# State read then routed attention on one core: z leaves its bank in one multiplication, mask and zeros share a tile, and a new order table

## The chip, the cores and the metric

The kernel runs on one core of a Trainium2 chip. Five queues work side by side: PE (matmuls), DVE and ACT (elementwise work; both read the matmul banks), POOL (elementwise work between on-chip tiles) and SP, which issues the DMAs. The metric is device microseconds (us) of one execution. Before the change the median of three runs is 297.14 us (296.94 to 297.83). The profile is of one further execution that took 296.96 us.

## The reference

```python
# x: 8 batches x 8 heads x 512 tokens x 64; state: 8 x 8 x 32 x 64
a     = softmax(scale * x @ state.T);  xread = a @ state      # tokens read the state
a2    = softmax(scale * state @ x.T);  sread = a2 @ x         # the state reads the tokens
x     = concat([xread, sread])         # 8 batches, 544 tokens, 512 wide
logits = x @ w_gate                    # 4 experts; each token takes its best 2
w      = softmax over the two chosen logits
for e in range(4):                     # causal attention of width 64 per expert
    ye   = softmax(causal(scale * (x @ wq[e]) @ (x @ wk[e]).T)) @ (x @ wv[e]) @ wo[e]
    out += (w of expert e, 0 where it is not chosen) * ye
```

A token has two chosen experts, its two "slots". The kernel sorts them so that slot 0 holds expert 1, 2 or 3 and slot 1 holds expert 0, 1 or 2, and computes two softmax rows for a token instead of four.

## The kernel before

A batch goes through four kinds of work. The *front* computes the state softmax `eb` (row maximum `mb`, exponential, row sum `sbm`, product with its reciprocal), turns it into `at`, and forms the products `gs` of state and weights, the values `v`, the keys `kt`, the queries `qf`/`qh`/`qm`, the gate and its weights `wgt`. The *side* work computes the other softmax (`mr`, `m`, `e`, `a`, `a2t`) and the 32 state tokens. The *main* work goes through the four 128-token blocks i of the batch: `probs` computes the masked scores of both slots (`p`, `mx`), the exponentials, a high and a low half (`ph`) and a DMA that transposes them (`pt`). `reads` multiplies `pt` by `v` into one bank: 193 columns per slot, 192 for three experts and one column of row sums. From there `su` (row sums), its reciprocal and `c6` (named `c` in rows; weight over row sum, three columns per slot) follow, then `z`, its halves `zh`, a DMA transpose, the product with `wo_n`, and the store of `o`. A *tail* handles the state tokens of two batches. In the last batch three blocks turn z on PE (`ident,z`) and skip the DMA.

Every number is a high and a low 16-bit half, so most products are three matmuls. There are 32 `reads`, eight batches of four blocks.

In `reads` before the change, z is made in four instructions out of one bank. Lines 907 to 910 multiply slot 1 by its three weights (one DVE instruction, or three on ACT). Lines 911 and 912 multiply the third expert of slot 0 (ACT or DVE). Lines 913 to 915 multiply the other two of slot 0 and add them onto slot 1 (two DVE instructions). In rows, z is the tile `z6` until its halves are taken.

The order is not found at run time. The functions only record steps (class `Steps`); a step may have several ways, say DVE or ACT, and `run` emits all steps in the sequence of a stored table `ORDER`. That table holds the sequence of steps, the way of each, and the buffer slot of each tile. So every queue follows a fixed list, and an engine waits at the head of its list. `FILL` is a list of start times for single matmuls over a tile of zeros, which have no result anyone reads; the table puts them mostly near the start. All instructions are emitted from line 268.

Of the kernel before, what the change touches and what calls it, by code (L numbers as in the profile page):

```python
# [18 lines left out]
CFG = dict(FILL=(1.0, 1.4, 1.8, 2.2, 2.6, 3.0, 3.4, 3.8, 4.2, 4.6, 5.0, 5.4, 5.8, 6.2, 6.6, 7.0, 7.4, 7.8, 8.2, 8.6, 9.0, 9.4, 9.8, 10.2, 10.6, 11.0, 11.4, 11.8, 12.2, 12.6, 13.0, 13.4, 13.8, 14.2, 14.6, 15.0, 15.4, 15.8, 16.2, 16.6, 17.0,), RA=-1, RG=1, RV=2, RK=2, ZL=3, GP=1, PT=4, ZM=4, SM=4, QM=4, SIDE=32, FB=1, PX=1, PA=2, LB=1, xn=4, W0=-33, PACE=37.0, LAG=2,  # L19
# [1096 lines left out]
```

## Time and profile before

| | before |
|---|---|
| median of 3 runs | 297.14 us |
| profiled execution | 296.96 us |
| its span, first to last instruction | 295.2 us |
| PE busy | 279.0 us, 95% of the span |
| DVE busy | 251.6 us, 85% |
| ACT busy | 218.0 us, 74% |
| POOL busy | 173.3 us, 59% |
| granted TensorE clock | 1.00 in every slice |

The profiled execution has 1.76 us outside its span. Busy time says how long an engine was at work, whether or not anyone waited for it; the idle time before an instruction and its releaser say who was late.

### The profile page before, as it was taken

The numbers are of one execution on the slowest core, as the hardware profiler recorded it, in microseconds if no ns is written. First come the engines' busy times: TensorE is split into PE (matmuls) and PEld (weight loads), VectorE is DVE, ScalarE is ACT, GpSimd is POOL, SyncE is SP. The second block draws the span as 40 slices with busy tenths as digits, with TensorE's granted clock in tenths as the row PEclk, the third lists the DMA queues.
The fourth block names the chain that finished last, engine by engine and source line by source line (L and its number), as shares of the span: only waits on it lengthen the run. The fifth ranks groups of instructions, "written<-read, shape, count | busy, mean of one in ns | idle before, by whom it ended". The sixth has DMA issues, their size and how long they took to land. (4 is left out here: it accounts for less than half of the span.)

```text
span 295.2 us, 9038 instructions
## 1 busy us (share of the span) xinstructions
PE 279.0 (95%) x3318; PEld 185.3 (63%) x3318; DVE 251.6 (85%) x821; ACT 218.0 (74%) x611; POOL 173.3 (59%) x245
## 2 busy tenths in 40 slices
PE   7899899998899899999999999999999999999895
PEld 3755555665576557576665777665777667844753
DVE  2788999999799889998889999898899996798552
ACT  3877687996699798898869986998684636646442
POOL 5773644678793786797657988496627535213000
PEclk9999999999999999999999999999999999999999
DMA  6997999999899999999999999998998877649954
GB/s 184 247 194 128 192 196 193 203 195 205 156 214 205 163 173 205 219 194 246 168 212 203 195 203 163 179 218 160 159 236 144 118 189 100 109 115 176 180 201 178
DMA packets 165564, 54.01 MB, mean 183 GB/s; under 512 B 144400, under 2 KB 161040, under 8 KB 165520
## 3 DMA queue, kind: packets, MB, share of 16 engines
q1 hardware_dynamic: 165520, 53.44, 93.9%
q8 instruction: 26, 0.43, 0.6%
q14 instruction: 18, 0.15, 0.1%
HBM read 11.08 MB, written 8.91 MB: 68 GB/s over the span
## 5 line engine op out<-in xcount | busy, mean ns | idle before, releaser
L268 PE MATMUL bank<-gs,at 128*128 128x260 f16 (+3 forms) x368 | 50.9, 283 | 0.5 <-DVE mx L268 0.4
L268 PE MATMUL bank<-kt,qm 128*128 128x128 f16 (+7 forms) x384 | 45.5, 299 | 1.1 <-DVE gs L268 1.1
L268 PE MATMUL bank<-v,pt 128*128 128x193 f16 x480 | 44.5, 246 | 1.9 <-DMA pt<-ph 1.8
L268 PE MATMUL bank<-wo_n,z 128*128 128x512 f16 (+1 forms) x198 | 45.4, 373 | 0.0
L268 PEld LDWEIGHTS <-pt 128*128 128x128 f16 x480 | 40.0, 97 | 5.1 <-DMA pt<-ph 2.5
L268 POOL TENSOR_TENSOR ph<-p,ph 128x768 f16<-128x768 f32 (+1 forms) x18 | 33.0, 1834 | 13.1 <-DVE gs L268 4.3
L268 ACT ACTIVATE p<-p,mx 128x256 f32<-128x256 f32 (+3 forms) x64 | 33.6, 555 | 7.7 <-DVE mx L268 4.5
L268 PEld LDWEIGHTS <-at 128*128 128x128 f16 x336 | 31.7, 97 | 9.2 <-issue 2.1
L268 PEld LDWEIGHTS <-qm 128*128 128x128 f16 (+1 forms) x384 | 22.8, 96 | 20.6 <-issue 9.3
L268 PEld LDWEIGHTS <-z 128*128 128x128 f16 x198 | 18.5, 97 | 19.5 <-issue 1.6
L268 DVE CUSTOM_DVE_ANT_0 p<-bank,maskb 128x128 f32<-128x128 f32 (+3 forms) x64 | 28.8, 480 | 0.2
L268 ACT ACTIVATE z<-bank,c 128x64 f32<-128x64 f32 x75 | 19.5, 319 | 11.5 <-POOL c L268 4.6
L268 PE MATMUL bank<-at,gs 128*128 128x512 f16 (+1 forms) x92 | 24.3, 399 | 1.2 <-DVE eb L268 0.9
L268 POOL TENSOR_TENSOR qh<-qf,qh 128x768 f16<-128x768 f32 x12 | 19.9, 1661 | 6.3 <-ACT qh L268 3.5
L268 ACT ACTIVATE o<-bank 128x512 f32<-128x512 f32 (+1 forms) x29 | 16.7, 586 | 5.3 <-PE bank L268 5.2
L268 POOL TENSOR_TENSOR eb<-eb,sbm 128x512 f32<-128x512 f32 x14 | 15.3, 1099 | 7.9 <-PE bank L268 3.9
L268 DVE SCALAR_TENSOR_TENSOR z<-bank,c,z 128x64 f32<-128x64 f32 x64 | 16.5, 274 | 3.9 <-ACT z L268 2.8
L268 ACT ACTIVATE xh<-xn 128x512 f16<-128x512 f32 x32 | 19.4, 630 | 0.0
L268 POOL TENSOR_TENSOR zh<-z,zh 128x256 f16<-128x256 f32 x20 | 14.3, 714 | 8.6 <-ACT zh L268 4.4
L268 POOL TENSOR_TENSOR c<-su,wgt 128x6 f32<-128x6 f32 x24 | 6.1, 255 | 20.7 <-DVE su L268 16.2
L268 DVE SCALAR_TENSOR_TENSOR xh<-xn,xh 128x512 f16<-128x512 f32 x23 | 16.5, 719 | 0.2 <-ACT xh L268 0.2
L268 ACT ACTIVATE ph<-p 128x768 f16<-128x768 f32 (+1 forms) x15 | 13.9, 927 | 3.1 <-DMA pt<-ph 3.0
(222 smaller groups left out, 643.7 us busy)
## 6 DMA issues: line engine op xcount, KB each, us to landing
out_dram<-o SPq DMA_DIRECT2D x33, 256.0 KB, 2.7
xn<-in_x_dram SPq DMA_DIRECT2D x16, 512.0 KB, 4.8
sn<-in_state_dram SPq DMA_DIRECT2D x9, 64.0 KB, 3.8
p<-in_moe_wo_dram SPq DMA_DIRECT2D x4, 128.0 KB, 2.8
z<-zh SPq DMA_TRANSPOSE x29, 3.2
xT<-xh SPq DMA_TRANSPOSE x28, 3.3
p<-in_moe_wv_dram SPq DMA_DIRECT2D x1, 384.0 KB, 5.3
p<-in_moe_wk_dram SPq DMA_DIRECT2D x1, 384.0 KB, 6.3
```

What stands on the lines that cost most here:

```text
L268: f(**{k: v.ap() if isinstance(v, View) else v for k, v in kw.items()})
```

## The change

Four edits. (1) In `reads` both slots are multiplied by their weights in one instruction (DVE: 384 columns out of the bank; or ACT: six of 64 columns), and the two experts that both slots may hold are added inside the on-chip tile, 128 columns, on POOL or DVE. The expert order inside z turns by one place, so `wo` is loaded in its own order (two DMAs of 128 rows instead of four of 64) and the tail picks its columns one place further. (2) The mask tile becomes the last 128 columns of the zeros tile. (3) `FILL` has 34 entries instead of 41. (4) The order table is a new one for the whole program: sequence, ways and slots. The `maskb` step, `probs` and `tail` change in column numbers only.

```diff
--- before.py
+++ after.py
@@ -16,62 +16,60 @@
 ALU = mybir.AluOpType
 AX = mybir.AxisListType

-CFG = dict(FILL=(1.0, 1.4, 1.8,
...
-15.8, 16.2, 16.6, 17.0,), RA=-1, RG=1,
...
+CFG = dict(FILL=(1.0, 1.4, 1.8,
...
+13.0, 13.4, 13.8, 14.2,), RA=-1, RG=1,
...
            FRONT=1.5, FSPAN=1.0, TSPAN=1.3, TOFF=1.2, KT=3, p32=3, ph=2, at=1, et=1, gs=1, xh=4, a2=1, o=4, sn=1, qf=2,
            n_eb=1, n_e2=1, n_a2t=1, n_xt_tail=2, n_z32=3, n_z=2, n_zh=3, n_tq=1, n_tv=2, n_tpt=2, n_tz=2)
 ORDER = (
     (
-        "c-jruV`C5s6adico0p9(+jgsE+qP}HwrtzBZQHhOzxN}~htnL2
...
+        "c-jq@gO(5q6acSpwbf>8+ict0X4|%Hd$VoZwr$(Cjraax&Y77i
...
     ),
     (
...
     ),
 )
 MASK = -1e30
@@ -301,8 +299,10 @@
     st = Steps(nc, sb, psum)


-    zeros = const.tile([P, DM], BF16, name="zeros")
+    band = const.tile([P, DM + P], BF16, name="band")
+    zeros = band[:, :DM]
     nc.vector.memset(zeros, 0.0)
+    st.tags["maskb"] = [band]
     ident = const.tile([P, P], F32, name="ident")
     make_identity(nc, ident)
     identh = const.tile([P, P], F16, name="identh")
@@ -396,9 +396,9 @@

     def constants():

-        maskb = st.buf("maskb", [P, S], BF16)
-        fill(maskb, 0.0)
-        select(maskb[:, S - P:], ALU.is_ge, MASK, 0, [[-1, P]], 1)
+        maskb = st.buf("maskb", [P, DM + P], BF16)
+        fill(maskb[:, DM:], 0.0)
+        select(maskb[:, DM:], ALU.is_ge, MASK, 0, [[-1, P]], 1)

         rows = [(c, s, slice((2 * c + s) * NS, (2 * c + s + 1) * NS)) for c in range(NB) for s in range(2)]
         mtail = st.buf("mtail", [P, P], BF16)
@@ -484,8 +484,7 @@
     def load_wo(after):
         for pr in range(E // 2):
             wof = stage()
-            for h in range(2):
-                st.dma(wof[h * D:(h + 1) * D, :DM], wo[(2 * pr + 1 + h) % E], 0.4, after=after)
+            st.dma(wof[:, :DM], wo[2 * pr:2 * pr + 2].rearrange("e d m -> (e d) m"), 0.8, after=after)
             hi_lo(DM, wo_n[:, 0, pr, :], wo_n[:, 1, pr, :], wof[:, :DM], 256.0, psum=False)

     tz, e2s = {}, {}
@@ -871,7 +870,7 @@
         for k, i in enumerate(unit):
             for s in range(2):
                 o = 2 * at_[i] + s * w_[i]
-                masked(w_[i], p32[:, o:o + w_[i]], part[s, i], consts["maskb"][:, S - w_[i]:], mx[:, 2 * k + s:2 * k + s + 1])
+                masked(w_[i], p32[:, o:o + w_[i]], part[s, i], consts["maskb"][:, DM + P - w_[i]:], mx[:, 2 * k + s:2 * k + s + 1])
         shifted(2 * nb, mx)
         for k, i in enumerate(unit):
             for s in range(2):
@@ -887,7 +886,7 @@
     def reads(b, i):
         v, w6 = vs[b], c6s.pop((b, i))
         pt, k0 = pts.pop((b, i))
-        z32 = st.buf("z6", [P, E * D], F32, bufs=CFG["n_z32"])
+        z6 = st.buf("z6", [P, 2, 3 * D], F32, bufs=CFG["n_z32"])

         zp = bank("zp")
         W = 3 * D
@@ -895,24 +894,21 @@
         for s in range(2):
             g += chain((zp[:, s * (W + 1):(s + 1) * (W + 1)], pt[:, c, k0 + s * (i + 1) + j, :], v[:, a, j, V0 - s + (1 - s) * D:V0 + 1 - s + (1 - s) * D + W])
                        for j in range(i + 1) for a, c in PROD)
-        st.mm(g, (len(g), W + 1, 128, 1), into=[z32])
+        st.mm(g, (len(g), W + 1, 128, 1), into=[z6])
         su = st.buf("su", [P, 2], F32, bufs=4)
         c6 = st.buf("c6", [P, 2, 3], F32, bufs=4)
         tiny(2, su, zp[:, W:W + 2], EPS * 2.0 ** 15)
         dve(28, nc.vector.reciprocal, out=su, in_=su)
         pair(6, out=c6, in0=su.unsqueeze(2).broadcast_to([P, 2, 3]), in1=w6.rearrange("p (s e) -> p s e", s=2), op=ALU.mult)

-        r = [zp[:, :W], zp[:, W + 2:2 * W + 2]]
-        o = z32[:, :W]
-        st.either([("DVE", 0.264, (nc.vector.tensor_tensor, dict(out=o.rearrange("p (e d) -> p e d", e=3), in0=r[1].rearrange("p (e d) -> p e d", e=3),
-                                                                in1=c6[:, 1, :].unsqueeze(2).broadcast_to([P, 3, D]), op=ALU.mult))),
-                   ("ACT", 0.595, *((nc.scalar.activation, dict(out=z32[:, e * D:(e + 1) * D], in_=r[1][:, e * D:(e + 1) * D],
-                                                               func=AF.Copy, scale=c6[:, 1, e:e + 1])) for e in range(3)))])
-        st.either([("ACT", 0.2, (nc.scalar.activation, dict(out=z32[:, W:], in_=r[0][:, 2 * D:], func=AF.Copy, scale=c6[:, 0, 2:3]))),
-                   ("DVE", 0.2, (nc.vector.tensor_scalar, dict(out=z32[:, W:], in0=r[0][:, 2 * D:], scalar1=c6[:, 0, 2:3], scalar2=None, op0=ALU.mult)))])
-        for e in range(2):
-            o = z32[:, (e + 1) * D:(e + 2) * D]
-            dve(D, nc.vector.scalar_tensor_tensor, out=o, in0=r[0][:, e * D:(e + 1) * D], scalar=c6[:, 0, e:e + 1], in1=o, op0=ALU.mult, op1=ALU.add)
+        by = "p s (e d) -> p s e d"
+        st.either([("DVE", 0.465, (nc.vector.tensor_tensor, dict(out=z6.rearrange(by, e=3), in0=zp.windows((W + 2, 2), (D, 3), (1, D)),
+                                                                in1=c6.unsqueeze(3).broadcast_to([P, 2, 3, D]), op=ALU.mult))),
+                   ("ACT", 1.19, *((nc.scalar.activation, dict(out=z6[:, s, e * D:(e + 1) * D], in_=zp[:, s * (W + 2) + e * D:s * (W + 2) + (e + 1) * D],
+                                                              func=AF.Copy, scale=c6[:, s, e:e + 1])) for s in range(2) for e in range(3)))])
+        kw = dict(out=z6[:, 1, D:], in0=z6[:, 1, D:], in1=z6[:, 0, :2 * D], op=ALU.add)
+        st.either([("POOL", 0.39, (nc.gpsimd.tensor_tensor, kw)), ("DVE", 0.2, (nc.vector.tensor_tensor, kw))])
+        z32 = z6.rearrange("p s c -> p (s c)")[:, 2 * D:]
         z = st.buf("z", [P, 2, 2, P], F16, bufs=CFG["n_z"])
         if b == B - 1 and i < CFG["ZL"]:

@@ -1047,7 +1043,7 @@
         zt = bank("zt")
         g = []
         for e in range(E):
-            o = e * D
+            o = (e + E - 1) % E * D
             g.append((zt[e % 2 * D:(e % 2 + 1) * D, e // 2 * N:(e // 2 + 1) * N].rearrange("p (n c) -> p n c", c=NB), zr[:, o:o + D],
                       consts["both"].rearrange("p (c n) -> p n c", c=NB), True, True))
         st.mm(g, (4, 4 * N, 128, 2), into=part)
```

What the new table does to the instruction counts (rows of each queue counted by kind, before and after): DVE has 50 instructions fewer, ACT 7, POOL 3, SP 2, PE the 7 zeros matmuls with their weight loads; PE's other matmuls are the same. The 32 z blocks were made by 64 scalar-tensor-tensor, 15 tensor-tensor of 192 columns and 8 tensor-scalar instructions on DVE and 75 on ACT; now by 22 tensor-tensor of 384 columns on DVE, 60 on ACT (ten blocks), and 32 additions, 18 on DVE and 14 on POOL.

The DVE queue at the start, in the first batch's front, before the change (`eb` is the state softmax, `sbm` its row sums, `mr` and `m` the row maxima of the other softmax, `gs` the gate and value products):

```order
L268 TENSOR_REDUCE sbm_120<-eb_116 128x16
L268 TENSOR_REDUCE mr_150<-bank_80 128x2
L268 TENSOR_REDUCE mr_150<-bank_81 128x2
L268 TENSOR_SCALAR sbm_120<-sbm_120 128x16
L268 RECIPROCAL sbm_120<-sbm_120 128x16
L268 TENSOR_TENSOR m_1_147<-mr_150 128x2
L268 TENSOR_REDUCE sbm_120<-eb_116 128x16
L268 SCALAR_TENSOR_TENSOR xh_96<-xn_87,xh_96 128x512
L268 TENSOR_SCALAR gs_122<-bank_83 128x260
L268 SCALAR_TENSOR_TENSOR wn_75<-p_1_114,wn_75 128x4x64
L268 TENSOR_SCALAR gs_122<-bank_77 128x260
L268 RECIPROCAL sbm_120<-sbm_120 128x16
```

The same place after the change:

```order
L266 TENSOR_REDUCE mr_149<-bank_83 128x2
L266 TENSOR_REDUCE mr_149<-bank_78 128x2
L266 TENSOR_TENSOR m_1_146<-mr_149 128x2
L266 TENSOR_REDUCE sbm_118<-eb_115 128x16 x2
L266 RECIPROCAL sbm_118<-sbm_118 128x16
L266 TENSOR_SCALAR sbm_118<-sbm_118 128x16
L266 TENSOR_SCALAR gs_121<-bank_80 128x260
L266 TENSOR_SCALAR gs_121<-bank_84 128x260
L266 RECIPROCAL sbm_118<-sbm_118 128x16
L266 TENSOR_TENSOR eb_115<-eb_115,sbm_118 128x512
```

The two maxima reductions moved ahead of both row sums, the second `xh` and a `wn` step moved behind, and the second product of `eb` with its reciprocal, on POOL before, is now on DVE. On PE both pairs of `eb` turns stand next to each other; before, six zeros matmuls and two products stood between them.

The DVE queue in the last batch, where the last blocks leave their banks, before the change (`z_0` to `z_2` are the z6 buffers, `tz` and `tzr` belong to the tail):

```order
L268 RECIPROCAL su_171<-su_171 128x2
L268 RECIPROCAL tsu_200<-tsu_200 128x1
L268 TENSOR_TENSOR tzr_205<-bank_82,tc_1_207 128x256
L268 RECIPROCAL su_169<-su_169 128x2
L268 SCALAR_TENSOR_TENSOR z_0_165<-bank_78,c_1_173,z_0_165 128x64
L268 TENSOR_SCALAR z_2_167<-bank_84,c_2_174 128x64
L268 SCALAR_TENSOR_TENSOR z_177<-bank_77,z_177 128x256
L268 SCALAR_TENSOR_TENSOR z_0_165<-bank_78,c_1_173,z_0_165 128x64
L268 SCALAR_TENSOR_TENSOR z_2_167<-bank_84,c_2_174,z_2_167 128x64 x2
```

And after it:

```order
L266 RECIPROCAL su_169<-su_169 128x2
L266 TENSOR_TENSOR c_1_172<-su_169,wgt_125 128x6
L266 SCALAR_TENSOR_TENSOR tz_208<-bank_81,tz_208 128x64x2
L266 TENSOR_TENSOR z_2_166<-bank_82,c_1_172 128x384
L266 TENSOR_SCALAR su_170<-bank_78 128x2
L266 TENSOR_TENSOR z_2_166<-z_2_166 128x128
L266 TENSOR_TENSOR z_1_165<-bank_77,c_3_174 128x384
L266 RECIPROCAL su_170<-su_170 128x2
L266 TENSOR_TENSOR c_3_174<-su_170,wgt_125 128x6
L266 TENSOR_TENSOR z_2_166<-bank_78,c_3_174 128x384
L266 TENSOR_TENSOR z_2_166<-z_2_166 128x128
```

DVE now makes z of a block alone, in two rows, where ACT and DVE took turns at one bank before.

## Rows read from the trace of the kernel before

**Rows 1.** Windows: head, middle, end; busy us (count) of each engine, PE clock, DMA.

```profile
core 0: us, PE busy (x) PEld busy (x) DVE busy (x) ACT busy (x) POOL busy (x), PEclk, DMA share, GB/s
0.00:45.00 45.00, 41.07 (x522) 24.65 (x522) 35.09 (x90) 31.69 (x74) 25.97 (x64) 1.00 0.96 191
45.00:240.00 195.00, 187.70 (x2339) 126.82 (x2338) 179.74 (x597) 159.01 (x449) 135.87 (x163) 1.00 1.01 188
240.00:295.20 55.20, 50.27 (x464) 33.84 (x458) 36.81 (x136) 27.28 (x89) 11.43 (x20) 1.00 0.71 160
```

**Rows 2.** Waits of PE in 45 to 240 us: total, times, longest.

```profile
PE bank L268 <- DVE gs L268: 1.3, 2, 1.1
PE bank L268 <- DMA a2t<-a: 1.2, 1, 1.2
...
PE bank L268 <- ACT z L268: 0.6, 1, 0.6
```

**Rows 3.** Groups by form: count, busy us, mean ns, idle before and releasers.

```profile
L268 ACT ACTIVATE z<-bank,c 128x64 f32<-128x64 f32 x75 | 19.5, 319 | 11.5 <-POOL c L268 4.6 <-DVE z L268 4.0 <-DVE c L268 2.9
L268 DVE SCALAR_TENSOR_TENSOR z<-bank,c,z 128x64 f32<-128x64 f32 x64 | 16.5, 274 | 3.9 <-ACT z L268 2.8 <-issue 0.7
...
L268 POOL TENSOR_TENSOR zh<-z,zh 128x256 f16<-128x256 f32 x20 | 14.3, 714 | 8.6 <-ACT zh L268 4.4 <-issue 3.5
L268 DVE TENSOR_TENSOR qf<-bank,m 128x384 f32<-128x384 f32 x26 | 13.6, 545 | 0.3
...
L268 POOL TENSOR_TENSOR c<-su,wgt 128x6 f32<-128x6 f32 x24 | 6.1, 255 | 20.7 <-DVE su L268 16.2 <-DVE tsu L268 4.0 <-DVE gt L268 0.4
L268 DVE TENSOR_TENSOR z<-bank,c 128x192 f32<-128x192 f32 x15 | 5.2, 348 | 1.1 <-ACT z L268 0.7 <-POOL c L268 0.4
...
L268 DVE TENSOR_SCALAR z<-bank,c 128x64 f32<-128x64 f32 x8 | 2.2, 279 | 0.2
...
L268 DVE TENSOR_TENSOR c<-su,wgt 128x6 f32<-128x6 f32 x8 | 1.8, 225 | 0.2
...
L268 DVE TENSOR_TENSOR eb<-eb,sbm 128x512 f32<-128x512 f32 x2 | 1.4, 684 | 0.0
```

**Rows 4.** PE in order of time, head: start us, us, idle before and releaser.

```profile
15.02 2.97 PE L268 MATMUL bank<-zeros 128*128 128x512 bf16 x13
18.40 0.66 PE L268 MATMUL bank<-ident,eb 128*128 128x128 f32 x4 [0.41 <-POOL eb L268]
...
21.27 0.66 PE L268 MATMUL bank<-ident,eb 128*128 128x128 f32 x4
```

**Rows 5.** POOL in order of time, head.

```profile
20.16 1.05 POOL L268 TENSOR_TENSOR eb<-eb,sbm 128x512 f32<-128x512 f32 x1 [0.34 <-DVE sbm L268]
```

**Rows 6.** DVE in order of time, head.

```profile
17.04 0.10 DVE L268 TENSOR_TENSOR m<-mr 128x2 f32<-128x2 f32 x1
...
17.65 1.25 DVE L268 SCALAR_TENSOR_TENSOR xh<-xn,xh 128x512 f16<-128x512 f32 x1
...
20.74 0.49 DVE L268 TENSOR_TENSOR s<-er 128x2 f32<-128x2 f32 x1 [0.66 <-ACT e L268]
```

**Rows 7.** The chain that ended last, one block of the last batch.

```profile
276.21 0.18 DVE c L268
...
276.49 0.32 ACT z L268
...
276.91 0.37 DVE z L268
...
277.81 0.29 DVE zh L268
```

**Rows 8.** Waits of PE in the last batch, in order of time.

```profile
273.60 3.68 PE L268 MATMUL bank<-v,pt 128*128 128x193 f16 x42 [1.04 <-DMA pt<-ph]
...
281.01 0.58 PE L268 MATMUL bank<-ident,z 128*128 128x128 f32 x2 [0.34 <-DVE z L268]
```

**Rows 9.** The halves of z on DVE: ns min, median, max; first and last start.

```profile
L268 DVE TENSOR_TENSOR zh<-z,zh x9: 396/417/426, 125.2 to 278.1; 128x256 f16<-128x256 f32 x9
```

More of the change, by code (lines that the diff above doesn't have):

```diff
@@ L69 @@
[L69 to L74 removed]
+        "c-jq@gO(5q6acSpwbf>8+ict0X4|%Hd$VoZwr$(Cjraax&Y77ikPPxdQb-B;AQ(zQey9)0p%8>(L)Z-f2m}lQ3I+}tAq(t<RFD<+K_<ussi8"
@@ new lines @@
+        "5Xhs=-`!a;b5009sYvO^=-18E=^<bZV00&+u6D2nAV543~|*b17!UFZx~p*3`YI#3tdKqV{z_n-_^g$!^Xib7W?2c_U3Jb<=P3<^LBs09z99"
+        "Xy3d5E%j?3PgoIPz}1lV`vYLpgVMczR(Q%!4oKh(I7g+fS3>qVnZB=3-KU6bcCAF1A0Pb>;;{mIF!WU@C*t<b0~{Vp*MuWC3p_?U^EngvhV^"
+        "9K^1%nwV^sxf>KxvC%{Rl4A<Zl6vsGp9!lUTNB{{T5hRBGa2Q_0Bp3r@;V7JeBQOHSK}8${17IMWgNYCZAut#g!v#17Q(*>7gCQ^zPQxr157"
+        "XfUEP?ef8|J`Sm<#)19$bW_P!89^P?!%3U?D7m)vyM(KxupfTVWe)fMxI&*1;{<4kIBhZG;2x4vxbpsD_(x2W*0>cpJ9iPS^~?U^8yV9XJ`P"
+        "<8qh+v1kj{z^!-(8saXfiLG%3G{T+O0ItAF2+zB)7QTnw*ckWVDo6rB@CBM+3fhacu|1}wBy=4vLkDb%!4yOtu?{9A!XHo<Q_**5gJ0nre1M"
@@ new lines @@
+        "<u8=7G<`UUkcDgA{26s(Voe;_$E$3(Ob|3L#(bnJwQX+O5W8vmo#8M|Q@Y>5Z3Eq2B3*aKT(KWvBP!7w65;KBF_`r`l$hlug0Cw_+bG!(;Q0"
+        "*Ztqus7a-D?9`T;zvkLy)X>NV`LnIV{rlw!*SRLC*nvvh?8(K4#)H~1qb0&oQ9bx5U1l>oPm9DCPw8&xC|HLIy{1DC>k%p$h;g^V+LA^5ikm"
+        "7qFI=hVsjjh&WCUf#=sT064Ox<T#xxF9~GdCG!NtQ2AqviaSq1BRTv8cc`k0m*mx8RQXGuIB`6C`p!t{%qhU$PN)ssv591_CileX;Ex^$j9f"
+        "Pqn+=PXA46{*Oj7^g%8OFox6q7IGDU8B7C_SFQoK%R8V`(~xh3PcL$Fo?5&fyfggSqGm7NPTa216)0=B8L&7>d$W%tK`<175&;c$G6^Bf5)u"
+        "=^9p`a+C`zQVPt37x6lVQe&D*O{hHGzyQ9)32++CrQBGIB61#VO3mpK=EdTa86)w1yovcR9zVoploG2^7L3og@B!ANAWq7)XgVd}L|mV0Py@"
@@ new lines @@
+        "<}y(t4H<n&yVQeiOX$2ydlE5bZVh)K9E-NuZZjH^?3u1$UDDfZy`l!+5zCF)Bjr6)I}8I%o^b1$w;nYjQy!xUT)t56HN$*J)<R;3r%n`cr5c"
+        "!@13CC{cu+?HBVJL*TR=?=fbTYN(9^J~n)?dc;v!Z+B4I#5Tt%bn;Groqls2tQ*N>Pla*8$ICcn3cQJZ5~8}sSm%!{xp=nVqgA?sdylz=EOL"
+        "Rde9K+$D^qi^`vh&oEFeyUPvS99xtL1G=RoXVO&ge=sW(yZ2XXyP!7z_VFYxIM^S$+f@ydxEhVI7M3kE!;{_SOPxuKgr?kwJkH=9SzAQqs=$"
+        "gF4m6VS2^I5shgLnm9<}0$3-eU;n;2XS(a`Je}%SwZJHLaniyoYk}TG~qmcpx|7b@Yta(+_^mFZd-l<bqt7chf8W$=BsAH|1aany*R`-bE3p"
+        "ob03W@`fwOZ!W|e=p7%RMqHl%a9XS=#rZu4&>?EZQ*}Ru@Im^^MnCWaN2Fuam=9A4jzpE@oJ6K0^pTI#Pdq_4<f3e((tMIOQ79MXe_WD_@p&"
@@ new lines @@
+        "r46}T*a;%a=9HdA%3$d&mspQ0)pNaeV)RN|_9Nu0j$X{sVM_zczjUre?5BApkM+T4=2P&lf?Tj`WspeWRuPfK0CM3<?m)Z_YGihto1YR+e5i"
+        "Z<Y{+=4ssZ;VQ9xD%hHZ`_e1NGr~Xow+TmM5FI~Q@U_FCP^&e<d&G+mf8|tx-v_9zAH)PDpeB^mpAeO?@1(iD*@7tlSo9#CHLhTy_5GcUmr?"
+        "!c_23^w?vk_5-fKlk4(~=R8wxz9IYio_#EA)N0LwOP%?QeGxdY~!5WfZa_U{mrMWe>T&E{AjE8c38NrM69tFu08P50VDaDb562^fNSLW(yo~"
+        "09b3_qZeoJU9TSbjzyD4s-@=QPX~Xaadbd3795;*YY8qDmr}r`u^Fzod^elb_0D{v@Ah2R)PLGM+zEG<hLWB)NQ{hm=AV>ujCPf9NZ{q8Rdx"
+        "X7M9>P5CsXe5W^*M(W5*iB4%Hm86sWx<q42YMIKhq=>|z^zxT}PzEU^|0ttm65u(US*Gb+&LSlxt1Q%PQb6W0azQCBpJfUcmbdgp3g~prAt9"
@@ new lines @@
+        "CuVb9?sy|kC{oL<(8cm)sfa$epmdL{o4m9M(;"
+    ),
+    (
+        "c-p;{(XPWV2tzsi|3_bSYHq*~mZwFUnxv@4U_7&5F5g?8AJ2nymlk@$ay$~2&qPc<cr5@c%GVV!7AuJF&TY=P(%wOwjuFL90GQNH^NeNAjI<"
+        "DN1^loew83<Lxj3I`Y5f<F`T=jY-Xa~S(cRS6_}Jh6J|e2}m@21C2p@RbNH0gYsQTi9@G5$_>LG<xLkrUIrV;f?7iV2Y*8NnI`^UujqNT`ed"
+        "84m1%7|bKm-P<b1m{sA3$p04>mQd+6tkX&57ef5*|6kDu{Qx>JFZnHcQt*6zlcG&MCwjU5GfFE>}G<RHQ$ZDPxattf72%c8~"
+    ),
+    (
+        "c-l>qi*7?P2t#@2|NnT$aHlPms)QPB4DJ4R;_tX;4#zmIue5l3`FA`B6D@oBfIaI9!cMrnlsP;i!N$1WDlwKFo9}{F@Oa^nrXM7e5E|N_#Ml"
+        "Hiz}hrv4e>L5+OB9j6#k^LU3Z<C5_4|JdepNH;i&<axqfz-GRqg^A~gb0Cy%dcn{<CI%!LMJ<zv?&+DUOaHOnPfdX{bLt2%U-r6dB!OY!nnG"
+        "rVF=F|n@tU!w`go9e9#BkhI#>hMaTE74>9zA33To>Cj=nLhL*OEnvQra__ora|#g1=*5zbv^to8fVw=Q85ki8==omWd}@_W)&wInf}x%W;cb"
+        "`-t8FaxvlLU`N5fD$cc9$=GyC&Z9ARX3XAhzyCt|*A$O9}NxNGt);yYInvnW&t$bA*IC>2}cjE@$zC=qP=jXdA^(_e_q%^6tL}TJXj|MxdT8"
+        "twL0qC|$?OOz(xc9ui72q#seeL)C6<kYS=XPn3>jY1rXj_kw^XOHk?)u{TEy?YA3nNZunLmCC23`"
```

64 lines of the change are left out of this document (16 added, 48 removed).

## The prediction

> **What bounds the kernel now.** I read the windows by stage first, then PE's waits, then the groups by form, and last the two ends in order of time. The windows [rows 1] show the reader three stages. In the middle, 45 to 240 us, PE is busy 187.70 of 195.00 us and DVE 179.74 (92%); PE stands still for 7.3 us and DVE for 15.3. So PE sets the time there, with DVE close behind. In the head PE is busy 41.07 of 45 us, but part of that is zeros matmuls, which fill time in which it would wait: 13 of them stand in one row of 2.97 us, 0.228 us each, and it waits 0.41 us more behind them [rows 4]. The head is a chain of latencies. In the last batch PE waits at two places of which one is z [rows 8]. PE's waits in the middle have many releasers; the two that bear on this change are DVE with 1.3 us over gs and ACT with 0.6 over z [rows 2].
>
> **z, on the three engines.** Before, DVE spends 64 x 0.274 + 15 x 0.348 + 8 x 0.279 = 17.5 + 5.2 + 2.2 = 25.0 us on z [rows 3]. After, 22 blocks cost one multiplication of 384 columns out of a bank. The query step has the same form, 0.545 us, so 12.0 us. The addition (128 columns, both inputs on chip) isn't in the trace. On DVE it lies between the tensor-tensor of 6 columns, 0.225 us, and that of 256, 0.415 [rows 3]; on the straight line between them 0.32, which I take: 18 x 0.32 = 5.8 (4.1 to 7.5). DVE falls by 25.0 - 17.8 = 7.2 us (5.5 to 8.9). ACT falls by 15 of its 75 pieces of 0.319 us, 4.8 us. POOL gains 14 additions between 0.255 us (6 columns) and 0.714 (256 columns) [rows 3]; on the line 0.48, so 6.7 us (3.6 to 10.0). POOL is busy 135.87 of 195 us in the middle [rows 1] and has that room. The other steps that change engine I cost at nothing in sum, since what leaves one engine lands on another with room.
>
> The readers of the bank also stop taking turns. In one block of the last batch [rows 7] c ends at 276.39 us, ACT makes one piece from 276.49, DVE one from 276.91, DVE two more, and z is ready at 277.81: 1.42 us. Made by DVE alone it takes 0.545 + 0.32 = 0.87 us, 0.55 less. On ACT six pieces of 0.319 plus an addition are 2.2 to 2.6 us, so ten of the 32 blocks get longer. In the groups, DVE's z pieces waited 2.8 us for ACT and ACT's 4.0 for DVE [rows 3].
>
> **Middle: -2.1 us.** Some 28 of the 32 blocks lie in it, so DVE's load falls by 28/32 x 7.2 = 6.3 us and its free time rises from 15.3 to 21.6. My estimate lets PE's waits shrink as that free time grows: 7.3 x (1 - 15.3/21.6) = 2.1. The ends are -7.3 (no visible wait is left) and +5 (below, the port).
>
> **Head: -1.2 us.** The list of DVE shows the second product of the state softmax coming sooner. Before, DVE ran an xh step of 1.25 us between the second row sum and its reciprocal [rows 6], and POOL needed 1.05 us for the product [rows 5], so PE turned the second half at 21.27, 2.87 us after the first [rows 4]. The new list has xh behind and the product on DVE, 0.684 us [rows 3]: 1.25 + (1.05 - 0.68) = 1.6 us sooner. The seven zeros matmuls that go are 7 x 0.228 = 1.6 us as well, what PE would otherwise wait. They stood in front of late inputs and return nothing by themselves. I take 1.2, since the first half and the weights that PE needs beside it move less (0 to -2.0). What is late next is the copy of the turned half out of its bank. With the zeros gone PE may stand still a little more often; the granted clock is 1.00 in all three stages, waits included [rows 1], so I price that at nothing.
>
> **End: -0.5 us.** PE waited 0.34 us for z before a turn [rows 8], and the block chain is 0.55 shorter on DVE; the 1.04 us for the pt transfer I leave. Between +1.0 (the tail's own product is late in the new list, a z now stands before it) and -1.4 (both waits go).
>
> **Mask, zeros, wo: 0.** The mask step reads the same number of columns from another place. POOL's fill of it, 128 columns instead of 512, lies in the head, where POOL is busy 25.97 of 45 us [rows 1]. Two wo DMAs instead of four take two issues off SP; the data are needed only by the first product of z. If that cover were gone, later arrival would cost some tenths.
>
> **Sum.** Against the profiled execution of 296.96 us (span 295.2 and 1.76 around it; 0.18 below the median of 297.14): 296.96 - 1.2 - 2.1 - 0.5 = 293.2 us.
>
> **A rule against it.** A DVE instruction over two elements took 0.49 us at 20.74 and ended when POOL's product (20.16 to 21.21) did; one of the same size at 17.04 took 0.10 [rows 5, 6]. So a DVE instruction with two on-chip inputs can stand behind POOL. Before, z's additions had one input in the bank; now all 32 have both on chip. Against that, nine subtractions with two on-chip inputs on DVE took 396 to 426 ns, none stretched [rows 9]. The Trainium skill (SBUF — State Buffer, section Who interferes with whom) says that a DVE instruction with two SBUF inputs contends with a GpSimd one that reads SBUF, the loser blocking for the whole instruction. The two rows at 20 us agree with it and the nine do not show it. By that rule the additions would cost what the first rival says; by the nine rows, the sum above.
>
> **Rivals.** The port, slower: Each of DVE's 18 additions waits as that one did, 0.39 us (7.0 in all, which eats the 7.2 saved), and POOL's 14 hold DVE up for their own 6.7 us. Then DVE's free time in the middle falls to 15.3 - 28/32 x 6.7 = 9.4 us, PE's waits grow to 7.3 x 15.3/9.4 = 11.9, and the time is 296.96 - 1.2 - 0.5 + 4.6 = 299.9. It decides once the additions lose more than 7.2 us, 0.22 us each. For it: the 0.49 us. Against: the nine rows.
>
> The table does not do what it says: its waits may be no nearer to the real ones, and one fixed list of a queue then waits at its head where the old did not: PE, after one stall as long as its longest in the middle, 1.3 [rows 2], in each of three batches, and no gain there: 296.96 - 1.2 - 0.5 + 3.9 - 1.3 = 297.9. For it: the whole program was put in order again, and 8 us on DVE mean little if 1 us is lost now and then. Against: the work per engine falls.
>
> No change: PE is busy 96% of the middle; the same matmuls run, and what DVE saves turns into idle time of DVE. Zeros matmuls go where PE then waits. Only the end is left: 296.5. For it: PE's longest waits in the middle are for gs and for a transfer, not for z [rows 2].
>
> More: half the 7.3 us of waits go, and the head gives 2.0: 296.96 - 2.0 - 3.7 - 1.4 = 289.9, or less if short waits inside the rows shrink too.
>
> **How the numbers follow.** Chances: forecast 0.56 (290.5 to 296), more 0.10, no change 0.15, table 0.09, port 0.10. About 0.3% (0.9 us) is what can be told from no change. Faster takes the forecast and more, 0.66; same 0.15; slower 0.19. The range of 288.5 to 298.8 leaves out the far half of the port and the best of more.
>
> **What would show it.** Right: the second pair of eb turns within 1 us of the first; no ACT and DVE pieces of z out of one bank; z additions of 0.25 to 0.35 us on DVE; DVE's busy time in the middle down by 5 us or more; PE's waits there near 5 us. Wrong: additions of 0.6 us and more beside POOL's work, or new waits of PE above 1 us in the middle; and if DVE's busy time falls while PE's stays and its waits too, the third rival holds.

## The result and the profile after

The changed kernel takes 292.58 us in the median of 4 runs (291.49 to 294.35) against 297.1 for the kernel before on the same chip; the ratio is 0.9836, 95% interval 0.9803 to 0.987. The forecast was 293.2. The profiled execution, whose rows follow, is the longest of the four, 294.35 us with a span of 292.6; most of what it has more stands in one place, shown below.

The windows of the changed kernel, with the columns of [rows 1]:

```profile
0.00:45.00 45.00, 40.50 (x498) 25.15 (x502) 32.95 (x89) 34.05 (x84) 25.43 (x61) 1.00 0.97 190
45.00:240.00 195.00, 189.68 (x2363) 128.52 (x2362) 178.29 (x566) 165.41 (x453) 131.93 (x164) 0.99 1.02 190
240.00:292.60 52.60, 47.82 (x451) 31.72 (x449) 34.59 (x118) 23.91 (x69) 10.98 (x18) 1.00 0.72 160
```

PE stands still for 5.3 us in the middle instead of 7.3. But DVE's busy time there fell only from 179.74 to 178.29 us, and the granted clock is 0.99, not 1.00. Yet a window of fixed length holds more of a faster kernel's work (2363 matmuls here, 2339 before), so the load is better compared over the whole program: DVE is busy 245.8 us instead of 251.6, ACT 223.4 instead of 218.0, POOL 168.3 instead of 173.3. The new table gave ACT other steps, so it carries more although its part of z shrank.

The groups by form that belong to z, with the columns of [rows 3]:

```profile
L266 ACT ACTIVATE z<-bank,c 128x64 f32<-128x64 f32 x60 | 13.3, 324 | 2.5 <-POOL c L266 1.9 <-DVE c L266 0.6
L266 DVE TENSOR_TENSOR z<-bank,c 128x384 f32<-128x384 f32 x22 | 12.1, 551 | 0.5
...
L266 POOL TENSOR_TENSOR z<-z 128x128 f32<-128x128 f32 x14 | 6.8, 488 | 4.2 <-ACT z L266 2.3 <-DVE su L266 1.7
...
L266 DVE TENSOR_TENSOR z<-z 128x128 f32<-128x128 f32 x18 | 5.5, 305 | 0.1
```

All four terms are near their estimates: 551 ns (545 taken), 305 (320), 488 (480), and 60 ACT pieces. DVE spends 12.1 + 5.5 = 17.6 us on z where [rows 3] add up to 25.0. The idle time ahead of them changed more: before, DVE and ACT waited 2.8 and 4.0 us for each other at z, and now for nothing of the kind.

The waits of DVE and ACT in the middle, longest first: total, times, longest. Before:

```profile
DVE eb L268 <- ACT e L268: 2.0, 4, 0.8
DVE tv L268 <- ACT tv L268: 1.3, 1, 1.3
...
DVE p L268 <- PE bank L268: 0.4, 1, 0.4
...
ACT p L268 <- DVE mx L268: 2.7, 2, 1.9
ACT p L268 <- POOL mx L268: 2.6, 3, 1.5
```

After:

```profile
DVE p L266 <- PE bank L266: 6.7, 6, 3.9
DVE kt L266 <- ACT kt L266: 0.8, 3, 0.3
...
ACT o L266 <- PE bank L266: 3.7, 4, 1.3
ACT xh L266 <- PE bank L266: 3.2, 1, 3.2
ACT xt_tail L266 <- PE bank L266: 2.4, 2, 1.6
```

The releaser has turned. Before, the engines that empty the banks waited mostly for each other; now they wait more for PE's next bank. Summed over the middle, DVE and ACT wait 22.3 us for each other and 9.4 for PE's banks before, 12.1 and 22.5 after. The two longest waits after, 3.9 and 3.2 us, belong to the one late transfer shown next and are not the order's; in the kernel `swap` (below), whose profile has no late transfer there, the sums are 13.4 and 17.0. PE's waits for DVE and ACT fall from 4.0 us to 2.5, in `swap` to 1.8.

In the head, PE in order of time, as in [rows 4]:

```profile
18.89 1.19 PE L266 MATMUL bank<-ident,eb 128*128 128x128 f32 x8
...
33.36 0.75 PE L266 MATMUL bank<-bd,xT 64*128 64x32 f16 x47 [1.28 <-ACT v L266]
...
40.81 1.42 PE L266 MATMUL bank<-kt,qm 128*128 128x128 f16 x16
```

Both halves of eb turn in one row; the second begins near 19.5, some 1.8 us sooner than in [rows 4]. Part of it goes again at 33.36 to ACT's v, a wait that the old list did not have.

The one new long wait lies at 96.6 us; PE and SP in order of time:

```profile
93.49 1.28 SPq L266 DMA_TRANSPOSE a2t<-a  x1
...
96.36 0.27 PE L266 MATMUL bank<-ident,sn 128*128 128x128 f32 x1
...
98.78 2.54 PE L266 MATMUL bank<-a2t,xh 128*128 128x64 f16 x48 [2.15 <-DMA a2t<-a]
...
101.25 1.41 PE L266 MATMUL bank<-wn,bd 64*32 64x512 f16 x24
```

and in the windows around it:

```profile
95.00:99.00 4.00, 1.85 (x18) 0.91 (x16) 3.89 (x13) 3.13 (x10) 2.81 (x3) 1.00 1.29 122
99.00:103.00 4.00, 4.00 (x75) 2.73 (x73) 1.64 (x4) 1.57 (x4) 1.35 (x2) 0.57 1.18 248
```

PE waits 2.15 us for a transfer and starts 5.3 us after its issue, and then the granted clock falls to its lower level (1.2 of 2.4 GHz; 0.57 in the mean of 99 to 103 us): 48 matmuls a2t,xh take 2.54 us here and 1.57 in the kernel before. The runs of the changed kernel are of two kinds: 291.49 and 291.61 us at a mean clock of 1.000 and 0.998, 293.55 and 294.35 at 0.994.

### The profile page after: what moved, and what is told of

Its sections match the earlier page's. It is cut to its first block, busy times and chain, and to the rows that moved or that the text cites. A ratio compares the mean times of both kernels' runs of the same rounds, so it can differ in the third digit from the quotient of the medians.

```text
span 292.6 us, 8929 instructions
## 1 busy us (share of the span) xinstructions
PE 278.0 (95%) x3308; PEld 185.4 (63%) x3311; DVE 245.8 (84%) x771; ACT 223.4 (76%) x604; POOL 168.3 (58%) x242
## 4 chain that ended last, share of the span: by engine, by line
PE 70%; DVE 14%; ACT 8%; DMA 5%; issue 2%; POOL 0%; DVEq 0%; ACTq 0%; SPq 0%
PE bank L266 70%; ACT p L266 2%; DMA a2t<-a 2%; DMA out_dram<-o 2%; DVE qf L266 2%; DMA xn<-in_x_dram 1%; DVE p L266 1%; DVE sbm L266 1%; ACT e L266 1%; DVE ph L266 1%; DVE xh L266 1%; DVE eb L266 1%; DVE m L266 1%; DVE gs L266 1%; ACT at L266 1%
## 5 line engine op out<-in xcount | busy, mean ns | idle before, releaser
L266 PE MATMUL bank<-kt,qm 64*128 64x512 f16 (+7 forms) x384 | 45.9, 299 | 0.4 <-DVE gs L266 0.2
L266 ACT ACTIVATE p<-p,mx 128x384 f32<-128x384 f32 (+3 forms) x64 | 33.4, 555 | 2.9 <-POOL mx L266 2.4
L266 POOL TENSOR_TENSOR ph<-p,ph 128x768 f16<-128x768 f32 (+1 forms) x16 | 28.6, 1793 | 9.1 <-ACT lg L266 2.9
L266 DVE CUSTOM_DVE_ANT_0 p<-bank,band 128x256 f32<-128x256 f32 (+3 forms) x64 | 28.9, 481 | 4.9 <-PE bank L266 4.9
L266 POOL TENSOR_TENSOR zh<-z,zh 128x256 f16<-128x256 f32 x24 | 16.6, 696 | 12.5 <-ACT zh L266 8.7
L266 POOL TENSOR_TENSOR qh<-qf,qh 128x768 f16<-128x768 f32 x10 | 16.6, 1666 | 11.7 <-ACT qh L266 6.3
L266 ACT ACTIVATE ph<-p 128x768 f16<-128x768 f32 (+1 forms) x20 | 18.5, 924 | 0.5 <-DMA pt<-ph 0.4
L266 POOL TENSOR_TENSOR eb<-eb,sbm 128x512 f32<-128x512 f32 x14 | 14.9, 1067 | 6.5 <-DVE sbm L266 4.7
L266 PE MATMUL bank<-a2t,xh 128*128 128x64 f16 x384 | 13.5, 198 | 3.2 <-DMA a2t<-a 2.1
L266 DVE TENSOR_TENSOR qf<-bank,m 128x384 f32<-128x384 f32 x28 | 14.8, 549 | 1.8 <-PE bank L266 1.0
L266 PEld LDWEIGHTS <-xh 128*128 128x128 f16 x384 | 13.0, 101 | 4.4 <-DMA a2t<-a 2.4
```

The costliest lines, as they stand in the source:

```text
L266: f(**{k: v.ap() if isinstance(v, View) else v for k, v in kw.items()})
```

## The experiments

Times are medians; ratios are against the kernel before on the same chip, with the 95% interval. Theory and rivals changed on the way, so the letters of the expectations run on.

**Each half of the change alone.** First the new z in the old table:

```diff
 order of all other steps: as before
-four pieces of z (ACT and DVE)
+multiplication (22 DVE, 10 ACT) at the place of the old first piece
+addition (18 DVE, 14 POOL) at the place of the old last piece
```

> The changed way of z alone, in the old order table: 32 multiplications of 384 columns out of the bank (22 DVE, 10 ACT) and 32 additions (18 DVE, 14 POOL), each at the place where the old table had the first and the last of the four pieces of z; 41 zeros matmuls as before; the shared tile of zeros and mask stays in, because the larger z does not fit without it, and wo is loaded in its own order but still in four transfers. Theory A (what I hold now: most of the gain is the order table's, the z edit alone gives little, since the DVE in the middle lost only 1.45 us of busy time): 295.5 to 297.2 us, less than 1.5 under the kernel before. Rival B (the z edit carries the gain, as the prediction's largest term says, -7.2 us of DVE): 292.5 to 294 us. Both expect z on the DVE near 18 us instead of 25.0, and the second half of eb at its old place near 21.3 us on PE.

309.17 us, ratio 1.040 (1.0356 to 1.0444); five of the six executions lie from 307.71 to 309.73, the sixth took 963.69 us, which nothing here explains. Both theories fall: the half costs 12 us. The other half, the new table with the old z:

```diff
 order of all other steps, zeros, wo, tile: as after
-multiplication and addition of z
+four old pieces, all at the place of the multiplication
```

> Everything of the changed kernel (new table, 34 zeros, wo in two transfers, shared tile) but z in the four old pieces, on the engines they had, all standing where the one multiplication stands in the new table. Theory A (the table carries the gain): 292.5 to 294 us, within 1.5 us of the changed kernel; PE takes both halves of eb in one group near 19 us. Rival B (the z edit carries it): 296 to 298 us, with new PE waits for z and for the DVE of more than 3 us together after 45 us.

305.29 us, ratio 1.0286 (1.025 to 1.0321). Both fall again. The groups of this kernel show what the old pieces do when they stand together:

```profile
L266 ACT ACTIVATE z<-bank,c 128x64 f32<-128x64 f32 x75 | 18.2, 320 | 14.1 <-DVE z L266 9.1 <-DVE c L266 3.9 <-POOL c L266 1.1
...
L266 DVE SCALAR_TENSOR_TENSOR z<-bank,c,z 128x64 f32<-128x64 f32 x64 | 15.1, 278 | 18.6 <-ACT z L266 16.7 <-ACT lg L266 1.0 <-POOL m L266 0.9
```

DVE stands 16.7 us for ACT's pieces and ACT 9.1 for DVE's. And the first kernel shows something of the new z, in the group of its DVE additions:

```profile
L265 DVE TENSOR_TENSOR z<-z 128x128 f32<-128x128 f32 x18 | 9.4, 520 | 4.2 <-ACT z L265 4.2
```

520 ns instead of 305: the same instruction, at other places. Both kernels were then mended. The new z wholly on DVE, at places that DVE always had:

```diff
-multiplication 22 DVE, 10 ACT; addition 18 DVE, 14 POOL
+multiplication 32 DVE, at the place of the first accumulating piece
+addition 32 DVE, at the place of the second
```

> The new z alone in the old table once more (shared tile, wo in its own order, 41 zeros as before), but now without a wait between engines inside z: all 32 multiplications and all 32 additions on the DVE, at the places of the two old pieces that the DVE always had. By rows, DVE work for z becomes 32 x 0.55 + 32 x 0.28 = 26.6 us against 25.0 before, ACT work falls by 19.5. Theory C (the 12 us that the first try lost come from the two in-order engines waiting for each other at z, above all the DVE for six ACT pieces, and from additions that POOL's two-input instructions hold up): back to 295.5 to 299 us, and gains of the z edit are nothing without new places for the other steps. Rival D (z in two steps does not suit the old table at all, since the addition comes later than the last old piece): above 303 us. Rival B (the z edit gains by itself): below 294.

300.47 us, ratio 1.0100 (1.0074 to 1.0126). Most of the 12 us is gone; DVE's waits for ACT in the middle fell from 14.9 to 5.9 us. The edit moved engines and places together, so their shares are not told apart. The kernel stays 2.7 us above the kernel before and 1.5 above what C gave. B falls here too. The old z in the new table, spread:

```diff
-four pieces at the place of the multiplication
+pieces 1 and 2 at the multiplication
+pieces 3 and 4 at the addition (22) or just before the bank's next use (10)
```

> The changed kernel with z in the four old pieces again, but spread: the first two pieces where the multiplication stands, the two accumulating DVE pieces where the addition stands (22 of 32) or just before the bank's next use (10). Theory C (the 12 us over the changed kernel came from all four pieces standing at one place, so that the DVE waited for ACT): 294 to 299 us, DVE waits for ACT's pieces of z under 6 us instead of 16.7. Rival D (the new table needs the bank's early release and the shorter DVE work): above 302.

301.38 us, ratio 1.0123 (1.0096 to 1.015); between C and D. In some blocks of this kernel the last two pieces take the weights c of a later block, since the new table reuses c's buffer sooner; the instructions are the same. It leaves out the guard that keeps c for its last reader, so those blocks come out wrong; it is no version of the program, and only its time is read. The accumulating pieces' waits for ACT fell from 16.7 to 5.5 us as C said; PE now waits for the bank that the late pieces hold, 6.6 us in nine waits:

```profile
PE bank L266 <- DVE z L266: 6.6, 9, 1.4
```

That is D's part: the new table counts on the bank being free after one instruction.

**Which engine adds.** In the new table the ways alone were changed:

```diff
-additions of z: 18 DVE, 14 POOL
+additions of z: 32 DVE            (second kernel: 32 POOL)
```

> The changed kernel with all 32 additions of z on the DVE: 14 more there at 0.31 us, +4.3 us of DVE work; 14 fewer on POOL at 0.49, -6.8 us. If DVE work is on the path at the share by which the prediction cut its middle term (some 7.3 us of PE waits to 21.6 of work), the time rises by some 1 to 1.5 us, to 293.5 to 294. If the two engines' SBUF accesses hold each other up (the rival of the port), the additions on the DVE become shorter than 0.305 us and the time falls below 292. If neither, it stays within 0.7 us of the changed kernel (292.6).

> The changed kernel with all 32 additions of z on POOL: 18 fewer on the DVE at 0.305 us, -5.5 us of DVE work; 18 more on POOL at 0.49, +8.8 us, POOL then busy some 177 of 293 us. If DVE work is on the path (one us of time for three of work), the time falls by 1 to 2 us, to 290.5 to 291.5. If POOL's additions hold up DVE operations (the port), POOL additions get longer than 0.6 us or DVE ones do, and the time rises above 294. If neither engine is on the path, it stays within 0.7 us of 292.6.

291.10 us (0.9791, 0.9755 to 0.9826) with all on DVE, 292.99 (0.9855, 0.9816 to 0.9894) with all on POOL. The kernel with 9.8 us more DVE work for the additions is the one with the lower median; of the rest, four of the six POOL runs have a mean clock of 0.994 and one of the six DVE runs. At a clock of 0.999 and above the DVE runs lie from 290.06 to 291.41 and the POOL runs at 290.95 and 292.29. Over the whole program DVE is busy 248.3 us in the one profile and 243.7 in the other, both at a clock of 1.00, and the span is 0.8 us shorter where it is busier. So neither the load nor the port is worth more than about a microsecond here; the expectation that DVE's work costs a third of itself falls. Its other branches do not fit as put either: with all additions on DVE they take 307 ns, not less than 305, and the median is 1.5 us under the changed kernel's, though only 0.4 to 0.5 under that kernel's two runs with the kept clock.

**The wait at 96.6 us and the clock.** Once the wait was filled with work that came next, once with work of no use:

```diff
 PE, fourth a2t group
 1 ident,sn
+24 wn,bd                   (swap)      | +8 zeros    (fill_gap)
 48 a2t,xh
-24 wn,bd                   (swap)
```

> The changed kernel with one PE step moved: the 24 matmuls wn,bd that follow the fourth group of 48 a2t,xh matmuls go ahead of it, into the wait of 2.15 us for the DMA of a2t at 96.6 us. Theory E (PE's idle stretch is what is followed by the granted clock of 0.50 from 99 to 103 us, which costs some 1.8 us in about half of the executions): no run with a mean clock under 0.998, median 290.8 to 291.8, all runs within 1 us. Rival F (the clock falls there whatever PE does, or the late DMA is not the cause): about half of the runs at 0.994 as before, median 292.3 to 293.

291.52 us, ratio 0.9794 (0.9769 to 0.9818), all six runs at 0.998 or more. E holds for the clock, though the spread is 2.2 us and not 1.

> The changed kernel with eight more zeros matmuls (0.21 us each, 1.7 us in all) on PE just ahead of the fourth group of a2t,xh, where PE waited 2.15 us for the DMA; nothing else moves. Theory E (an idle PE is what the granted clock's fall follows): the DMA can be as late as before, but no run has a mean clock under 0.998, and the runs lie within 1.5 us of each other; median 291.5 to 293.3, since in executions with an early DMA the eight matmuls are 1.7 us of extra work. Rival F (the fall follows the late transfer, not the idle PE): a third to a half of the runs at 0.994, as in the kernels with the same order at that place (9 of 22 runs).

291.08 us, ratio 0.978 (0.9757 to 0.9804), all five runs at 0.998 or more, 290.52 to 291.76. PE of this kernel in order of time:

```profile
95.84 0.27 PE L265 MATMUL bank<-ident,sn 128*128 128x128 f32 x1
95.95 1.89 PE L265 MATMUL bank<-band 128*128 128x512 bf16 x7
97.67 1.56 PE L265 MATMUL bank<-a2t,xh 128*128 128x64 f16 x48
```

With useless matmuls in the place of the wait (eight, of which the trace holds seven) the kernel is some 1.6 us below the changed one by the two ratios, whose intervals just touch. Of the runs with new z, new table and nothing in the wait (the changed kernel and the two with moved additions) 7 of 16 have a mean clock of 0.994; with the wait filled (swap, fill_gap and best, below) none of 15 is under 0.998. The 9 of 22 of the expectation count the kernel with the old z pieces too, whose fall stands at another place.

The counts carry this, not the profiles. In the profiles of swap, fill_gap and both kernels with moved additions the transfer lands 3.2 to 3.3 us after its issue, against 5.2 in the profile of the changed kernel, and where nothing fills the place PE goes straight on. SP and PE of the kernel with all additions on DVE:

```profile
92.03 1.28 SPq L265 DMA_TRANSPOSE a2t<-a  x1
95.35 0.27 PE L265 MATMUL bank<-ident,sn 128*128 128x128 f32 x1
95.46 1.56 PE L265 MATMUL bank<-a2t,xh 128*128 128x64 f16 x48
```

So no trace shows a late transfer with its place filled. The kernels with moved additions, swap and fill_gap also ran on three different chips; that the transfer was merely late less often where the place was filled is not excluded, and why it is late at all stays open.

**Small edits and single moves in the old table.** Two tests of how the old table takes a change that costs no engine anything:

```diff
-zeros and mask in two tiles, 41 zeros matmuls
+one tile, 34 zeros matmuls (the last seven dropped)
```

> The kernel before with two of the small edits alone: the shared tile of zeros and mask, and 34 zeros matmuls instead of 41 (the last seven by place, which stand from 21 to 45 us, are dropped); z, wo and the order of all other steps stay. Theory G (the zeros only fill time in which PE waits): within 0.5 us of the kernel before, PE waits longer by what the seven took. Rival H (each dropped zeros matmul, 0.21 to 0.38 us of PE, shortens the first stage): 1.5 to 2.7 us faster.

299.01 us, ratio 1.0044 (1.0023 to 1.0065): slower than before, which neither theory gave. PE of this kernel in order of time:

```profile
43.40 0.61 PE L267 MATMUL bank<-gs,less 128*128 128x260 f16 x2 [0.74 <-DVE gs L267]
...
45.18 0.69 PE L267 MATMUL bank<-ident,eb 128*128 128x128 f32 x4 [0.55 <-DVE mx L267]
...
45.88 5.37 PE L267 MATMUL bank<-kt,qm 128*128 128x384 f16 x24
```

and its window behind the two waits:

```profile
45.00:49.00 4.00, 3.82 (x17) 1.66 (x17) 3.38 (x8) 3.81 (x12) 1.37 (x2) 0.58 1.04 199
```

In the kernel before, zeros stand in both waits and the clock there is 1.00; here it is 0.58. Three of twelve runs show it in their mean clock (0.994) and lie at 299.15 to 299.79; the nine others have a median of 298.73, so about 1.3 us comes from elsewhere and stays open.

```diff
 PE at 53 us          PE at 100 us
+24 bd,xT            +24 wn,bd
 2 v,less             48 a2t,xh
-24 bd,xT            -24 wn,bd
```

> The kernel before with two groups of PE matmuls moved and nothing else: 24 bd,xT ahead of the two groups v,less that waited 0.73 us for ACT's v at 53.3 us, and 24 wn,bd ahead of the 48 a2t,xh that waited 1.25 us for a DMA at 100.6. No engine gets less work and z stays as it was. Theory I (PE's waits in the middle are time on the path, whatever the DVE's load, so new places alone gain what they fill): 1.2 to 2.0 us faster than before. Rival J (a wait filled in the middle is given back at the next bank or DMA, and only less work on DVE or ACT would gain): within 0.5 us.

299.44 us, ratio 1.0059 (1.0037 to 1.0081). Both fall: the two waits are gone and others are longer. PE in order of time:

```profile
52.97 0.84 PE L267 MATMUL bank<-xT,bd 64*32 64x512 f16 x24 [0.52 <-DVE mx L267]
...
60.20 0.81 PE L267 MATMUL bank<-gs,at 128*128 128x256 f16 x6 [1.05 <-DVE qf L267]
68.37 1.78 PE L267 MATMUL bank<-kt,qm 128*128 128x128 f16 x24 [1.30 <-DMA qm<-qh]
...
78.27 2.17 PE L267 MATMUL bank<-v,pt 128*128 128x193 f16 x24 [1.26 <-DMA pt<-ph]
```

What was put behind came later at the engines after PE, and the next waits are for them and for a transfer. Before, the waits from 45 to 104 us were 4.0 us together; here 4.7. Which step carries the delay on was not followed link by link.

**The port.** The last test of the half that loses, with the additions taken off DVE:

```diff
-multiplication 32 DVE, addition 32 DVE
+multiplication 32 DVE, addition 32 POOL
```

> The earlier kernel with the new z wholly on the DVE in the old table (300.5 us, additions 449 ns in the mean instead of 280, each long one ending 0.14 us behind a POOL instruction with two inputs), now with the 32 additions on POOL. Theory K (the additions cost because the DVE stands still while POOL's instruction holds it up, 14.4 us of DVE time in all): 296 to 298.5 us. Rival L (what costs is that z comes later than in the old four pieces, on any engine): 300 us or more, since POOL's additions take 0.49 us and queue behind its other work.

301.32 us, ratio 1.0107 (1.0065 to 1.0149), against 1.0100 with them on DVE. K falls: 14.4 us off DVE do not bring the 2 to 4.5 us that it gave. But three of these four executions have a mean clock of 0.993 or 0.994; the one at 1.0 took 299.21 us, against 300.06 and 300.58 with the additions on DVE. So L holds in the median, and at an equal clock about a microsecond may have been bought, by one execution.

**A version better than both.**

```diff
+additions of z: 32 DVE
+24 wn,bd ahead of 48 a2t,xh at 96 us
+ACT: v ahead of qh at 31.4 us
```

> The changed kernel with three edits: all additions of z on the DVE, the 24 wn,bd matmuls ahead of the late a2t group, and in the first stage ACT's eviction of v one place earlier, ahead of the copy of qh for which ACT waited 0.55 us while PE waited 1.28 us for v at 32.3. Expected 289.2 to 290.3 us: 291.1 with the additions on the DVE, less about 1.0 of the 1.28 us wait. If the wait for v only turns into the next one (kt at 37.7), it stays at 290.5 to 291.5.

290.83 us, ratio 0.977 (0.9746 to 0.9793), all four runs at 1.0. PE in order of time:

```profile
31.84 0.75 PE L265 MATMUL bank<-bd,xT 64*128 64x32 f16 x47 [0.35 <-ACT v L265]
...
37.50 0.38 PE L265 MATMUL bank<-kt,less 128*128 128x512 f16 x1 [0.74 <-ACT kt L265]
```

The wait for v fell from 1.28 to 0.35 us, the next one, for kt, rose from 0.48 to 0.74, so the second branch of the expectation came true. The kernel is some 0.7% below the changed kernel by the two ratios. Of the 1.75 us between the two medians 1.0 is the kept clock; the move of v can't be told from nothing beside the kernel with all additions on DVE.

## Why the prediction was right, and where it was not

The time was right (292.58 for 293.2), in part by luck: in the two runs that kept the clock the kernel takes 291.5 us. Not all of the steps were right.

**z, on the three engines: right.** DVE's work on z fell by 7.4 us (7.2 said), each duration within 5%.

**Middle, -2.1 us: the mechanism was wrong, and the size fits by luck.** The step let PE's waits shrink as DVE's free time grows from 15.3 to 21.6 us. DVE's free time is 16.7 us, and PE's waits still fell to 5.3, of which 2.15 is the transfer. Where the clock is kept they fall further; the middle of swap, of all additions on DVE, and of all on POOL, with the columns of [rows 1]:

```profile
45.00:240.00 195.00, 191.67 (x2404) 130.32 (x2403) 181.19 (x580) 167.08 (x459) 131.13 (x164) 1.00 1.05 193
45.00:240.00 195.00, 191.76 (x2404) 130.24 (x2403) 183.02 (x590) 166.01 (x458) 126.68 (x154) 1.00 1.05 192
45.00:240.00 195.00, 191.16 (x2403) 130.11 (x2402) 179.39 (x564) 166.38 (x457) 139.08 (x177) 1.00 1.06 192
```

PE stands still for 3.2 to 3.8 us there, so the change gains some 3.5 to 4.1 us in the middle and not 2.1; the late transfer and the lower clock take part of it back in some executions. In the first two rows DVE has less free time than before and PE waits less than half as long. With 9.8 us of DVE work more or less for the additions the time stays within about a microsecond at equal clock. So DVE's load is not the term. What changed is who waits for whom, as the sums of waits show: the new order has banks emptied before PE wants them. I had called that list's merit doubtful and gave its failure a rival of its own.

**The sum of separate terms: wrong as a picture.** Neither half, as built here, gains by itself. With the new z alone the kernel is 1.0% to 4.0% slower, with the new table alone 1.2% to 2.9%, with both 1.6% faster. The places in these half kernels were chosen by hand, so the small ends, 2.7 and 3.6 us, are upper bounds of what a half must cost. What a table made in the new way for the old z would give was not tried, and so how much of the 4.5 us belongs to z and how much to the better order stays open; that z's form lets a table be better is supported by the 6.6 us that PE waits when the bank is held longer.

**Head, -1.2 us: nearly.** From the first bd,xT to the first kt,qm PE takes 32.0 us before (8.9 to 40.9), 31.2 in the profile after (9.6 to 40.8), 30.9 with all additions on DVE: 0.8 to 1.1 us. But this is not the same work: 24 wn,bd and one gs,less that the old list had ahead of that kt,qm, some 0.7 us there, stand behind it in the new one. Counted by finished matmuls instead (an estimate: each at the median distance between starts of its form in the kernel before, zeros left out), PE has done at 45 us of the old kernel what it does 0.9 us sooner in the profile after, and 1.3 to 2.1 us sooner in the kernels of the experiments that share the new z and table. So a gain of about the size said is likely; link by link it is not shown. What came late next was not the copy of the turned half but ACT's v, 1.28 us.

**End, -0.5 us: not seen as such.** PE stands still for 4.8 us from 240 us on, 4.9 before. The waits for pt and z [rows 8] are gone; one block on ACT takes their place. ACT and PE of the changed kernel in order of time:

```profile
272.46 1.34 ACT L266 ACTIVATE z<-bank,c 128x64 f32<-128x64 f32 x6 [1.36 <-POOL c L266]
...
273.82 1.47 PE L266 MATMUL bank<-wo_n,z 128*128 128x512 f16 x6 [1.63 <-ACT z L266]
```

That the ten blocks on ACT get longer was said; that one of them lies in the last batch was not.

**Zeros at nothing: wrong.** I priced PE standing still at nothing because the clock was 1.00 in all stages. The experiment with seven zeros fewer and the wait at 96.6 us show the price: a granted clock of about half for 3 to 4 us in a part of the executions. It is 0.9 us between the medians of the two kinds of runs there and 2.4 between those of the changed kernel, where the late transfer is part of it. The forecast had no such term; it cost the changed kernel 1 us in its median by the two kinds of runs.

**The port: real, but not here.** The rival's mechanism is in the traces (last section). The nine subtractions held against it [rows 9] could not speak: none of them began beside a running POOL instruction with two inputs. In the new table only one of 18 DVE additions runs into it, so 305 ns; in the old one at least 6 of 18 (520 ns) and 15 of 32 (449 ns). Even there the last port test leaves it a price of about a microsecond at most, so the 299.9 us of that rival had a true cause and a wrong price.

**The signs named.** Right: eb's pair, no shared banks, additions of 0.305 us, waits near 5 us. Wrong as said: DVE down by 5 us in the middle (1.45; the window holds more work, and over the whole program it is 5.8). And one of the signs against, a new PE wait above 1 us, came true without turning the result.

## What to carry to other kernels

When engines run fixed lists, the load of an engine that is 92% busy is not what its work costs: read who releases whom, and try a load up and down before giving a microsecond of it a price. A faster operation and the order made for it belong together; tried in each other's absence they can both lose, and a wait that is filled by a move can return wherever the delayed step heads a chain. Compare the load of two kernels over equal work, not over windows of equal length. Where a transfer can come late, try ready matmuls ahead of its reader, or useless ones if there are none: with the place filled, none of 15 runs here showed the lower clock, against 7 of 16.

## What the runs showed of the hardware

A DVE addition with both inputs in SBUF waits for a POOL instruction with two inputs that is already running. DVE and POOL in order of time, of the kernel with the new z on DVE in the old table:

```profile
125.10 1.64 POOL L265 TENSOR_TENSOR ph<-p,ph 128x768 f16<-128x768 f32 x1
125.53 1.36 DVE L265 TENSOR_TENSOR z<-z 128x128 f32<-128x128 f32 x1
```

The addition ends at 126.89, 0.15 us behind POOL's at 126.74. Of the 32 additions there 17 began beside such an instruction, and 15 of these ended 0.14 to 0.15 us behind it, after up to 1.36 us; the 15 others took 0.23 to 0.29. The remaining two, which were not held (0.27 and 0.29), began within 0.01 us of the start of POOL's instruction, and there POOL's took 0.13 us longer than its kind: 1.29 us at 81.46, for a median of 1.16, and 1.18 at 143.60, for 1.05. So the one that is already running goes on, and the other is late. The old accumulating pieces of the kernel before, with one input in the bank, show no such thing: 0.27 us in the mean for 37 that began beside such an instruction and 0.28 for the 27 others. The Trainium skill (SBUF — State Buffer, section Who interferes with whom) has this difference between two inputs in SBUF and one, and the trace agrees in both halves.

The granted clock fell to about half behind waits of PE of 2.15 us, of 2.02 (for pt, in the last port test), of 1.32 (for z, in the new table with the old z at one place), and of 0.74 and 0.55 us shortly after each other. It did not after every wait: behind 2.5 us for v in the first half kernel, 2.04 us for gs in the one with z on DVE, and 1.74 us in the spread one, it stayed at 1.00. What decides between them the runs don't show.
